# A burst's share of P @ V blocks in a two-branch attention kernel: from a rule on the queue's length to a rule on blocks left over runs left

## Chip, cores, metric

One core of a Trainium2 chip. The metric is device microseconds of one execution; before the change the median of 3 runs is 1779.55 us (1779.37 to 1779.65). Lower is better.

## What is computed

Two attention branches over the same 2048 x 512 input, mixed by a gate, in float32 throughout:

```python
x = A_x                                    # (1, 2048, 512), 32 heads of 16
g = sigmoid((x * gate_w).sum(-1, keepdims=True))
# branch A: softmax attention over all 2048 keys
a = (softmax(q @ k.T * 0.25) @ v) @ wo
# branch B: 4 segments of 512; causal softmax inside a segment,
# plus a linear memory M, z of the segments before it
o = sigmoid(beta) * (phi(q) @ M / (phi(q) @ z + 1e-6)) + (1 - sigmoid(beta)) * (softmax(causal logits) @ v)
b = o @ B_wo
return g * a + (1 - g) * b
```

## The kernel before, in words

**Two stages.** A first stage (up to about 300 us of the profile) makes the projections and the memory terms and leaves q, k and v of all heads in DRAM. The second stage is one loop over **slots**, written out by hand: the loop's order is the order of each engine's instructions.

**Units.** The work of the second stage is 64 units: a group of four heads and 512 queries, of branch A or B. Unit k (0 to 31) of A has 64 slots, that of B ten; they alternate (A 0, B 0, A 1, B 1, ...), 74 slots to a pair, 2368 slots in all. One slot of A is one head's 128 keys by 512 queries.

**What a slot n does**, in this order. `score_part` issues one score product `st<-qA,kA` on TensorE into one of three PSUM banks, and the exponential of it on ScalarE (`p<-st`), which writes a quarter of a tile `p` (128 keys, four heads, 512 queries). When four slots have filled such a tile, its four **blocks** (128 keys x 128 queries, four heads each) go into `queue`; for A they may be taken from slot n + 2 on (`GAP`). `max_part` works 96 slots ahead (`LEAD`): it makes the plain product `sm<-kA,qA` of a later unit into one of four PSUM banks (`banks[m % 4]`), and VectorE reduces it to the row maximum (`pm<-sm`, L226). For B it uses a masked reduce (L238, `rest<-sm,mask`), over one or two pieces to a slot. The softmax's shift is needed before a unit's scores can start, hence the lead.

**Bursts.** After every third slot (`BURST = 3`) comes the rest of TensorE's work: one of

- three products of `shared`, a list of the output projection and of later q tiles (about four bursts to a unit),
- or `some_values(n, most())`: P @ V blocks from the queue. `most()` says how many. Neighbouring blocks of one `p` tile are merged to a **run** of 128, 256, 384 or 512 columns: `ops<-p,vA`, four products (one to a head, in four column groups of the array; the profile counts eight records to a run). A run never goes beyond a `p` tile, so three blocks are one run or two (1+2, 2+1), four are 4, 1+3, 2+2 or 3+1.

So a burst on TensorE reads: three `st`, three `sm`, and the runs. Once to a pair of units a burst also carries the transposes of the maxima (`mt_ps<-identf,ms`, L196), which take one of the three score banks.

**The rule that the change touches**, L1008 to L1015. `ends` gives the shares by the number of blocks left near a unit's end (A: 9 left, take 3; 8, 4; 7, 3; 6, 3; 5, 5), and B's shares. Otherwise a burst takes 3, or 4 where `over` is true: the queue longer than `LOW = 3` by a share of `HIGH - LOW = 11` that shrinks with the unit's blocks left (for B: longer than 3). The last 94 slots (`wide`) and what follows them take up to 8 blocks at a time and do not ask the rule.

**Kinds of unit.** 74 slots are not a multiple of 3, so the bursts fall on a unit's slots in three ways, by k mod 3. Bursts of units with the same k mod 3 are alike; below, units 10, 11 and 12 stand for the three kinds (k mod 3 = 1, 2, 0), ten of each from unit 1 to unit 30.

Of the kernel before, what the change touches and what calls it, by code (L numbers as in the profile page):

```python
# [32 lines left out]
SLOTS = {"A": 64, "B": 10}  # L33
NU = 32
LEAD = 96
BURST = 3
LATER = (2, 3)
MOST = 3
LOW, HIGH = 3, 14
NP = 6  # L40
GAP = {"A": 2, "B": 5}
LATE_T = 9
# [5 lines left out]
def gated_mix(ctx, tc, x, xT, wqkv, a_wo, b_wq, b_wk, b_wv, b_wo, beta, gate_w, out):  # L48
# [55 lines left out]
    first = {}  # L104
# [5 lines left out]
    nS = len(slots)  # L110
# [138 lines left out]
    def run_todo(m):  # L249

        for e in [e for e in todo if e[0] <= m]:
            todo.remove(e)
            e[1]()

    def run_late(pool, tag, m):
        while us := [e for e in late if e[0] < m][:2]:
            for e in us:
                late.remove(e)
            transpose_max(us, pool, tag)
# [3 lines left out]
    def loads(m):  # L263

        m = min(m, len(maxs) - 1)
        while loaded[0] <= m:
            u, (r, i) = maxs[loaded[0]]
            if loaded[0] == first_max[u]:
                load_q(u)
            kc = u[2] if u[0] == "B" else i // 8  # L270
            if (u, kc) not in kt_:
                load_k(u, kc)
            loaded[0] += 1
# [383 lines left out]
    def later_tile(c, o):  # L657

        def done():
            full = fr.tile([128, CH], F32, tag="part", name="full")  # L660
            nc.scalar.copy(full, ops)
            t = fr.tile([128, 2, 2, 2, 128], F32R, tag="blk", name="qhalves", bufs=2)
            t = t.rearrange("p a o h t -> p a (o h t)")
            nc.gpsimd.tensor_copy(t[:, 0], full)
            nc.gpsimd.tensor_sub(t[:, 1], full, t[:, 0].bitcast(F32))
            for i in range(2):
                at(n + 12, lambda i=i: nc.sync.dma_start(
                    qd["A", o, c][16 * i:16 * i + 16].rearrange("d h t -> (d h) t"), raw(t[:, i])))


            if o == NO - 1 and c == LATER[0]:
                for i in range(2):
                    load_halves(("x", LATER[1]), "B", x_later(LATER[1]), (2 * i, 2 * i + 1), n + 2 + 18 * i,
                                [n + 24 + 29 * i, n + 28 + 29 * i])
            elif o == NO - 1:
                for i, (side, w) in enumerate((("A", a_wo), ("B", b_wo))):
                    load_halves(side, side, w, (0, 1), n + 2 + 18 * i, [n + 22 + 8 * i, n + 26 + 8 * i])
                    for k in range(2, 4):
                        load_halves(side, side, w, (k,), n + 50 + 22 * i + 3 * (k - 2), [n + 62 + 18 * i + 5 * (k - 2)])

        def f(i):
            k, (a, b) = i // 3, ((1, 0), (0, 1), (0, 0))[i % 3]
            assert {("q", k), (("x", c), k)} <= ready
            nc.tensor.matmul(ops, halved["q"][:, k, a, o * 128:(o + 1) * 128], halved["x", c][:, k, b],  # L684
                             start=(i == 0), stop=(i == 11))
            if i == 11:
                done()
        for i in range(12):
            yield lambda i=i: f(i)
# [30 lines left out]
    wide = range(nS - LEAD + 2, nS - 4)  # L720
    assert wide.start % (2 * BURST) == wide.stop % (2 * BURST) == 0

    def from_bank(n):

        return nc.vector.tensor_copy if n > wide.start + 4 else nc.scalar.copy

    queue = []

    def score_part(n):
# [38 lines left out]
        if j % 4 == 3 or j == SLOTS[side] - 1:  # L768
            if side == "B":
# [7 lines left out]
              + [(2, 0, 256), (2, 128, 384)])  # L777

    def some_values(n, most):

        taken = len(queue)
        while queue and most and queue[0][0] <= n:
            _, u, i = queue.pop(0)
            most -= 1
            side, g, c = u
            w = 1
            while (queue and most and queue[0][0] <= n and queue[0][1] == u and (i + w) // 4 == i // 4
                   and (side == "A" or PIECES[i + w][0] == PIECES[i][0])):
                queue.pop(0)
                most -= 1  # L790
                w += 1
            p = pt_[u, i // 4]
            if side == "A":
                c0 = q0 = 128 * (i % 4)
                v = vt[u][:, i // 16, i // 4 % 4]
            else:
                b, c0, q0 = PIECES[i]
                v = vt[u][:, b]
            done = i + w == SLOTS[side]
            for h in range(4):  # L800
                nc.tensor.matmul(ops[32 * h:32 * h + 17, q0:q0 + 128 * w], v[:, 17 * h:17 * h + 17], p[:, h, c0:c0 + 128 * w],  # L801
                                 start=(i == 0), stop=done, tile_position=(0, 32 * h))
            if done:
                raw = ob.tile([128, CH], F32, tag="o", name="oraw")
                from_bank(n)(raw, ops)
                nc.sync.dma_start(od[side, c][4 * g:4 * g + 4].rearrange("h r t -> (h r) t"), raw)
                stored.add(u)
                if side == "B" and c and g % 2 == 0:
                    octet("M", g // 2, c, n + 4)
                if (side, g ^ 1, c) in stored and u != ("A", NG - 1, NCH - 1):  # L810
                    octet(side, g // 2, c, n + (20 if side == "B" and (g < 5 or c < last) else 8))
                if u in between:
                    shared.extend(output(*between[u]))
                if side == "A" and c == 0:
                    shared.extend(later_tile(LATER[g // NO], g % NO))
                break
        return taken - len(queue)
# [117 lines left out]
    def output(c, b, pairs, then, ps=ops):  # L935

        ks = [(os, o, i) for os in pairs for o in os for i in range(2)]
        for k in ks:
            def f(n, k=k):
                os, o, i = k  # L940
                assert loaded_blocks[c, b, os] > len(blocks) - 2
                t = blocks[loaded_blocks[c, b, os] - 1][:, i, o % 2].unsqueeze(1)
                list(products(ps, t, 0, "AB"[i], o, k == ks[0], k == ks[-1]))[n]()
                if k == ks[-1] and n == 2:
                    then(ps, c, b)
            for n in range(3):
                yield lambda n=n, f=f: f(n)
# [57 lines left out]

    ends = {"A": {9: 3, 8: 4, 7: 3, 6: 3, 5: 5}, "B": {10: 3, 7: 3, 4: 4}}

    def most():  # L1008

        if not queue:  # L1010
            return 0
        side = queue[0][1][0]
        left = SLOTS[side] - queue[0][2]
        over = 64 * (len(queue) - LOW) > (HIGH - LOW) * (left if side == "A" else 0)
        return ends[side].get(left, MOST + over)  # L1015

    filled = [0]
    n = 0
    while n < nS or queue or beside or filled[0] < len(fill):
        for f in beside.pop(n, []):  # L1020
            f()
        if n < nS:
            score_part(n)
        m = n + LEAD
        if m < nS:
            loads(m + PRE)

            max_part(m, lambda: banks[m % 4])
        run_todo(m)
        if n >= nS or n % (2 * BURST if n in wide else BURST) == (2 * BURST if n in wide else BURST) - 1:  # L1030
            taken = 0
            if shared:
                for _ in range(3):
                    shared.pop(0)()
            else:
                taken = some_values(n, 8 if n >= nS or n in wide else most())
            if n < 5:


                for i in range(4):  # L1040
                    nc.tensor.matmul(ops[:, 128 * i:128 * i + 128], identf, identf, start=True, stop=True)
            if any(e[0] < m + 1 for e in late):
                run_late(st_ps, "st", m + 1)
            else:

                for _ in range(0 if n >= nS and queue else 4 if n not in wide else 11 - taken if taken < 8 else 0):
                    if filled[0] == len(fill) or fill[filled[0]][0] > n:
                        break
                    fill[filled[0]][1]()
                    filled[0] += 1  # L1050
        n += 1
# [45 lines left out]
```

## Time and profile before

| | |
|---|---|
| median of 3 runs | 1779.55 us (1779.37 to 1779.65) |
| profiled execution, its own time | 1779.57 us |
| its span, first to last instruction | 1777.8 us |
| PE (TensorE matmul) busy | 1770.5 us, 14945 records |
| PEld (weight loads) busy | 915.2 us |
| DVE (VectorE) busy | 1573.5 us |
| ACT (ScalarE) busy | 1435.4 us |
| POOL (GpSimd) busy | 641.2 us |
| granted TensorE clock | 1.000 |

The span is 1.8 us shorter than the execution's time; the profiled execution lies 0.02 us from the median. "Busy" is the union of an engine's instructions in time. Matmuls overlap each other, and so do VectorE's reduces (one starts before the last has written its result), so a row "4.27 ... x7" says that seven reduces took 4.27 us from the first one's start to the last one's end. In rows of the timeline the first number is the start of a group in us, the second its length, and "x" the number of instructions merged in it.

### The profile page before, as it was taken

The page shows a single profiled execution, that of the slowest core. Times are in us where ns is not written, and L with a number is a line of the kernel's source. Part 1 is how long each engine was busy: PE and PEld are TensorE (multiplying, and loading weights), DVE is VectorE, ACT ScalarE, POOL GpSimd, SP SyncE. Part 2 cuts the span into 40 slices and gives each one's busy share as a digit, 9 for nine tenths or more (in the row PEclk, how much of TensorE's full clock was granted, in tenths as well). Part 3 has the DMA queues.
Part 4 walks back from the last instruction along what each step waited for, and adds up shares of the span by engine and source line. Part 5 has one row for each costly group of instructions (what it writes and reads, how often), then busy time and mean ns, then how long its engine had stood idle before and what let it go on. Part 6 is the DMA issues. An engine that isn't in the chain of part 4 may idle for free.

```text
span 1777.8 us, 40673 instructions
## 1 busy us (share of the span) xinstructions
PE 1770.5 (100%) x14945; PEld 915.2 (51%) x14945; DVE 1573.5 (89%) x3331; ACT 1435.4 (81%) x2752; POOL 641.2 (36%) x748
## 2 busy tenths in 40 slices
PE   9999999999999999999999999999999999999999
PEld 8887776444444444444444444444444444444444
DVE  4236777999999999999999999999999999999931
ACT  5455445888888888888888888888888888888884
POOL 3002223415161417443434343344434253435343
PEclk9999999999999999999999999999999999999999
DMA  7667566445453536555454544454545353544542
GB/s 251 212 234 239 182 205 187 121 110 134 128 152 107 147 108 179 143 146 128 132 143 121 145 127 146 128 146 126 147 112 154 113 141 116 150 119 138 144 160 62
DMA packets 141270, 261.55 MB, mean 147 GB/s; under 512 B 36328, under 2 KB 58888, under 8 KB 140560
## 3 DMA queue, kind: packets, MB, share of 16 engines
q1 hardware_dynamic: 139712, 257.55, 50.3%
q8 instruction: 119, 1.95, 0.5%
q0 software_dynamic: 1216, 1.14, 0.3%
q14 instruction: 79, 0.65, 0.1%
q10 hardware_dynamic: 144, 0.26, 0.0%
HBM read 174.39 MB, written 83.25 MB: 145 GB/s over the span
## 4 chain that ended last, share of the span: by engine, by line
PE 95%; DVE 1%; ACT 1%; DMA 1%; POOL 1%; issue 0%; SPq 0%; POOLq 0%; DVEq 0%
PE ops L801 33%; PE st L744 27%; PE sm L205 14%; PE pr L311 10%; PE ops L913 4%; PE ops L684 2%; PE sm L913 2%; PE num L514 1%; POOL mn L378 1%; PE pr L401 1%; PE mps L545 0%; DVE pm L226 0%; DMA qdB<-q 0%; PE mt_ps L196 0%; DMA raw<-xT 0%; PE sm L744 0%
## 5 line engine op out<-in xcount | busy, mean ns | idle before, releaser
L767 ACT ACTIVATE p<-st 128x512 f32<-128x512 f32 x2261 | 1189.5, 601 | 152.3 <-PE sm L205 108.2
L226 DVE TENSOR_REDUCE pm<-sm 128x1 f32<-128x512 f32 x2048 | 1281.1, 683 | 11.5 <-PE sm L205 11.3
L744 PE MATMUL st<-qA,kA 50*128 50x512 f32 x2014 | 663.4, 432 | 0.0
L205 PE MATMUL sm<-kA,qA 48*128 48x512 f32 x2048 | 660.4, 428 | 0.4
L801 PE MATMUL ops<-p,vA 128*17 128x128 f32 (+3 forms) x6432 | 552.0, 442 | 0.0
L744 PEld LDWEIGHTS st<-qA,kA 50*128 50x128 f32 x2014 | 328.0, 185 | 415.1 <-ACT p L767 370.6
L205 PEld LDWEIGHTS sm<-kA,qA 48*128 48x128 f32 x2048 | 331.7, 185 | 16.9 <-issue 4.6
L863 POOL TENSOR_TENSOR rcp<-rec,minus 128x32 f32<-128x32 f32 x43 | 234.2, 5446 | 76.4 <-DMA rec<-dend 71.8
L238 DVE CUSTOM_DVE_ANT_0 rest<-sm,mask 128x128 f32<-128x128 f32 (+3 forms) x512 | 247.3, 483 | 1.4
L801 PEld LDWEIGHTS ops<-p,vA 128*17 128x17 f32 x6432 | 130.5, 96 | 214.4 <-issue 189.4
L748 POOL TENSOR_SCALAR_AFFINE_SELECT p<-p 128x512 f32<-128x512 f32 x128 | 79.4, 636 | 324.9 <-ACT p L767 320.4
L205 PE MATMUL sm<-kB,qB 48*128 48x128 f32 (+3 forms) x512 | 166.2, 385 | 0.0
L744 PE MATMUL st<-qB,kB 50*128 50x512 f32 (+1 forms) x495 | 109.3, 330 | 0.3 <-ACT mt L199 0.3
L381 DVE TENSOR_TENSOR q<-full,q 128x512 fp32r<-128x512 f32 x56 | 38.6, 689 | 74.9 <-ACT q L374 67.9
L744 PEld LDWEIGHTS st<-qB,kB 50*128 50x128 f32 x495 | 69.9, 186 | 59.3 <-ACT p L767 48.6
L801 PE MATMUL ops<-p,vB 128*17 128x128 f32 (+3 forms) x1504 | 87.5, 350 | 0.0
L205 PEld LDWEIGHTS sm<-kB,qB 48*128 48x128 f32 x512 | 80.0, 184 | 0.0
L187 POOL CAST ms<-nm 128x16 fp32r<-128x16 f32 x32 | 6.3, 196 | 201.5 <-DVE nm L183 199.6
L378 POOL TENSOR_SCALAR mn<-full 128x512 f32<-128x512 f32 x24 | 36.4, 1515 | 102.5 <-ACT full L373 82.2
L373 ACT COPY full<-pr 128x512 f32<-128x512 f32 x56 | 32.8, 586 | 40.2 <-PE pr L311 37.3
L187 POOL CAST ms<-pm 128x16 fp32r<-128x16 f32 x32 | 6.3, 196 | 127.9 <-DVE pm L238 127.8
L801 PEld LDWEIGHTS ops<-p,vB 128*17 128x17 f32 x1504 | 33.1, 97 | 31.1 <-issue 26.6
(198 smaller groups left out, 1622.7 us busy)
## 6 DMA issues: line engine op xcount, KB each, us to landing
kA<-kdA SPq DMA_DIRECT2D x256, 128.0 KB
vA<-vdA SPq DMA_DIRECT2D x31, 544.0 KB
kA<-kdA SPq DMA_DIRECT2D x256, 64.0 KB
kdA<-q SPq DMA_DIRECT2D x32, 256.0 KB
qdB<-q SPq DMA_DIRECT2D x32, 256.0 KB
qA<-qdA SPq DMA_DIRECT2D x64, 128.0 KB
kdB<-q SPq DMA_DIRECT2D x32, 256.0 KB
qB<-qdB SPq DMA_DIRECT2D x64, 128.0 KB
```

The source lines that it names most:

```text
L205: nc.tensor.matmul(ps[:, n0:n0 + n], rows(qt[u][:, :, s * 128:(s + 1) * 128], h, 48), rows(k[:, :, k0:k0 + n], h, 48), start=True, stop=True)
L226: nc.vector.tensor_reduce(pm[:, h, s, kc:kc + 1], ps, axis=AX.X, op=ALU.max)
L238: rows_left.append(lambda h=h, s=s, n0=n0, w=w: nc.vector.tensor_tensor_reduce(out=tri["rest"][:, 0:w], in0=ps[:, n0:n0 + w], in1=tri["mas ...
L311: nc.tensor.matmul(ps, l(a, k), r(b, k), start=(n == 0), stop=(n == 11))
L378: nc.gpsimd.tensor_scalar_min(ph["mn"], full, 0.0)
L381: nc.vector.tensor_sub(q2, full, q1.bitcast(F32))
L744: nc.tensor.matmul(ps[:, n0:n0 + CH - q0], rows(k[:, :, b * 128:(b + 1) * 128], h, 50), rows(q[:, :, q0:], h, 50), start=True, stop=True)
L748: nc.gpsimd.affine_select(out=x, in_=x, pattern=[[0, 4], [1, 128]], base=0, channel_multiplier=-1, compare_op=ALU.is_ge, fill=0.0)
L767: nc.scalar.activation(p[:, h], ps, AF.Exp, scale=SCALE)
L801: nc.tensor.matmul(ops[32 * h:32 * h + 17, q0:q0 + 128 * w], v[:, 17 * h:17 * h + 17], p[:, h, c0:c0 + 128 * w], start=(i == 0), stop=done ...
L863: eng.tensor_tensor(r, rec, minus, op=ALU.pow)
L913: yield lambda i=i, x=x, w=w: nc.tensor.matmul(ps, t[:, b, x], halved[side][:, o, w], start=start and i == 0, stop=stop and i == 2)
```

## The change

`most` now gets the slot n. For a unit of A it counts the bursts left until the unit's blocks should be done (`runs`, from the unit's first slot, its 64 slots and the gap) and takes four blocks where the blocks left but four are at least 3.5 times these bursts, and where more than six blocks (`due`) will have come in by the next burst, or it is the last. Else it takes three. The table `ends` holds only for B and when no burst is left, so for A it hardly applies any more. For B the share is as before. `HIGH` goes.

```diff
-LOW, HIGH = 3, 14
+LOW = 3
...
-    def most():
+    def most(n):
 
         if not queue:
             return 0
-        side = queue[0][1][0]
-        left = SLOTS[side] - queue[0][2]
-        over = 64 * (len(queue) - LOW) > (HIGH - LOW) * (left if side == "A" else 0)
-        return ends[side].get(left, MOST + over)
+        _, u, done = queue[0]
+        side, left = u[0], SLOTS[u[0]] - done
+        runs = (first[u] + SLOTS[side] + GAP[side] + 1 - n) // BURST
+        if side == "B" or runs < 1:
+            return ends[side].get(left, MOST + (len(queue) > LOW))
+        due = min(SLOTS[side], (n + BURST - GAP[side] - first[u] + 1) // 4 * 4) - done
+        return MOST + (left - 4 >= (MOST + 0.5) * runs and (due > 2 * MOST or runs == 1))
...
-                taken = some_values(n, 8 if n >= nS or n in wide else most())
+                taken = some_values(n, 8 if n >= nS or n in wide else most(n))
```

On ScalarE, VectorE, GpSimd and in the DMA queue of SyncE every instruction stands where it stood; only names of buffers and source lines differ. On TensorE the score products, the products for the maxima, the transposes, `shared` and B's runs stay in their bursts, and only the division of A's blocks among the bursts changes. Blocks per P @ V burst of A, in order ("t": the burst with the transposes):

| unit | before | after |
|---|---|---|
| 10 | 4 3 4 4 4 3 3 4 4 3 4 4 4t 3 3 2 4 4 | 4 4 3 4 3 4 3 4 3 4 3 4 3t 4 3 3 4 4 |
| 11 | 4 4 3 4 4 4 3 4 4 4 3 4 3t 4 3 3 2 4 | 4 4 3 4 3 4 3 4 3 4 3 4 3t 4 3 4 3 4 |
| 12 | 4 4 4 4 4 4 4 3 4 4 4 3t 3 3 4 4 4 | 4 4 4 4 4 4 4 4 4 3 4 3t 3 3 4 4 4 |

Over the whole loop up to `wide`, A's bursts of four go from 351 to 330, of three from 174 to 216, of two from 21 to 1 (547 bursts before and after). Its runs go from 220, 208, 168 and 208 (of 512, 384, 256 and 128 columns; 804 in all) to 229, 189, 188 and 189 (795).

TensorE in unit 11, from the fourth of its bursts above to the fifth (`st` scores of the running unit, `sm` products for the maxima of later ones, `ops` the runs); before:

```order
L801 MATMUL ops<-p,vA 17x128 x4
L801 MATMUL ops<-p,vA 17x384 x4
L744 MATMUL st<-qA_8967,kA_197 128x512
L205 MATMUL sm_3008<-kB_201,qB_9666 128x512
L744 MATMUL st<-qA_8967,kA_197 128x512
L205 MATMUL sm_3009<-kA_195,qA_9598 128x512
L744 MATMUL st<-qA_8967,kA_197 128x512
L205 MATMUL sm_3010<-kA_195,qA_9598 128x512
L801 MATMUL ops<-p,vA 17x128 x4
L801 MATMUL ops<-p,vA 17x384 x4
```

The same place after the change:

```order
L801 MATMUL ops<-p,vA 17x128 x4
L801 MATMUL ops<-p,vA 17x384 x4
L744 MATMUL st<-qA_8967,kA_197 128x512
L205 MATMUL sm_3008<-kB_201,qB_9654 128x512
L744 MATMUL st<-qA_8967,kA_197 128x512
L205 MATMUL sm_3009<-kA_195,qA_9586 128x512
L744 MATMUL st<-qA_8967,kA_197 128x512
L205 MATMUL sm_3010<-kA_195,qA_9586 128x512
L801 MATMUL ops<-p,vA 17x128 x4
L801 MATMUL ops<-p,vA 17x256 x4
```

The burst's second run has 256 columns in place of 384: three blocks, where there were four.

TensorE near the end of unit 11, its last burst but two and its last but one (the second `sm` of the piece belongs to B's maxima); before:

```order
L801 MATMUL ops<-p,vA 17x128 x4
L801 MATMUL ops<-p,vA 17x256 x4
L744 MATMUL st<-qA_8967,kA_199 128x512
L205 MATMUL sm_3008<-kB_200,qB_10319 128x256 x2
L744 MATMUL st<-qA_8967,kA_199 128x512
L205 MATMUL sm_3009<-kA_197,qA_10238 128x512
L744 MATMUL st<-qB_9666,kB_201 128x512
L205 MATMUL sm_3010<-kA_197,qA_10238 128x512
L801 MATMUL ops<-p,vA 17x256 x4
```

After:

```order
L801 MATMUL ops<-p,vA 17x384 x4
L801 MATMUL ops<-p,vA 17x128 x4
L744 MATMUL st<-qA_8967,kA_199 128x512
L205 MATMUL sm_3008<-kB_200,qB_10315 128x256 x2
L744 MATMUL st<-qA_8967,kA_199 128x512
L205 MATMUL sm_3009<-kA_197,qA_10234 128x512
L744 MATMUL st<-qB_9654,kB_201 128x512
L205 MATMUL sm_3010<-kA_197,qA_10234 128x512
L801 MATMUL ops<-p,vA 17x384 x4
```

The first burst of the piece grows from three blocks to four, the last from two to three: here the blocks go that were taken out of the bursts in the middle of the unit.

## The prediction

> **What bounds the kernel now.** I read the busy time by stretches first (PE, PEld, DVE, ACT, POOL, each with its instructions, then granted clock, DMA share, GB/s):
>
> ```profile
> 120.00:300.00 180.00, 179.01 (x844) 130.80 (x843) 126.04 (x239) 86.87 (x153) 45.00 (x42) 1.00 0.63 208
> ...
> 400.00:600.00 200.00, 199.97 (x1888) 91.29 (x1890) 199.80 (x423) 176.77 (x343) 74.24 (x90) 1.00 0.50 133
> ...
> 1400.00:1600.00 200.00, 200.00 (x1887) 91.39 (x1886) 199.74 (x423) 177.17 (x344) 82.01 (x92) 1.00 0.50 133
> 1600.00:1660.00 60.00, 60.00 (x580) 27.27 (x576) 59.89 (x123) 52.77 (x103) 24.32 (x28) 1.00 0.50 144
> ```
>
> In the slot loop both PE and DVE read 100%, so this view cannot say which of them sets the pace; ACT (88%) and the weight loads (46%) do not. Next I read the timeline of PE in unit 11 for the price of a burst, from the start of its runs to the next `st`, and from one first `st` to the next.
>
> ```profile
> 816.63 0.50 PE L744 MATMUL st<-qA,kA 50*128 50x512 f32 x1
> ...
> 817.53 0.84 PE L801 MATMUL ops<-p,vA 128*17 128x384 f32 x8
> 818.30 0.50 PE L744 MATMUL st<-qA,kA 50*128 50x512 f32 x1
> ...
> 819.28 1.06 PE L801 MATMUL ops<-p,vA 128*17 128x128 f32 x16
> 820.27 0.50 PE L744 MATMUL st<-qA,kA 50*128 50x512 f32 x1
> ...
> 824.95 0.85 PE L801 MATMUL ops<-p,vA 128*17 128x128 f32 x16
> 825.72 0.49 PE L744 MATMUL st<-qA,kA 50*128 50x512 f32 x1
> ...
> 826.65 1.06 PE L801 MATMUL ops<-p,vA 128*17 128x256 f32 x16
> 827.64 0.50 PE L744 MATMUL st<-qA,kA 50*128 50x512 f32 x1
> ```
>
> Three blocks in one run take 0.77 us (817.53 to 818.30), as 1+2 too 0.77 (824.95 to 825.72); four as 1+3 take 0.99 (819.28 to 820.27), as 2+2 again 0.99. So **the price goes by blocks, about 0.22 us each, and hardly by runs**. From `st` to `st` a burst of three costs 1.67 us (816.63 to 818.30), one of four 1.92 (825.72 to 827.64).
>
> Then the timeline of DVE in the same unit:
>
> ```profile
> 819.62 1.28 DVE L226 TENSOR_REDUCE pm<-sm 128x1 f32<-128x512 f32 x2
> 820.84 0.69 DVE L238 CUSTOM_DVE_ANT_0 rest<-sm,mask 128x512 f32<-128x512 f32 x1
> ...
> 821.46 9.91 DVE L226 TENSOR_REDUCE pm<-sm 128x1 f32<-128x512 f32 x16
> ...
> 831.41 4.27 DVE L226 TENSOR_REDUCE pm<-sm 128x1 f32<-128x512 f32 x7
> 835.68 0.29 DVE L238 CUSTOM_DVE_ANT_0 rest<-sm,mask 128x128 f32<-128x128 f32 x1
> ```
>
> One reduce lasts 0.69 us, but seven last 4.27: their starts lie (4.27 - 0.69) / 6 = 0.597 apart. That is DVE's own pace, 1.79 us for three, between PE's 1.67 and 1.92. Sixteen at that pace would last 0.69 + 15 x 0.597 = 9.65; they last 9.91. DVE was **starved for 0.26 us inside a row that shows it busy throughout**, because the tail of one reduce covers the wait for the next. That is what bounds the loop: DVE at its pace, plus such starved stretches where PE comes with bursts of four and has no lead left. The four `sm` banks are the lead: a burst of four eats 0.13 of it, one of three gives 0.12 back. In unit 11 the sequence before is 4 3 4 4 4 3 4 4 4 over this stretch.
>
> **The change, part by part.** Nothing is added and no other engine's order moves; A's blocks go to other bursts. TensorE's sum is the same: 42 more bursts of three, 21 fewer of four and 21 fewer of two, and 0.22 us a block makes that nothing. What counts is where a four stands on spent lead.
>
> *Unit 11's kind.* Starved now: 0.26 in the row of sixteen; and seven reduces from 831.41 should end their turn at 831.41 + 7 x 0.597 = 835.59, but the next starts at 835.68: 0.09. Together 0.35. After the change fours and threes alternate from the third burst on, so each four (-0.13) meets a three (+0.12) before it, and the lead entering the stretch, which fed the first fours, is kept. Both waits go. What was moved out goes into its last bursts but two and but one, 3 2 becoming 4 3. The 0.02 at 820.84 (1.22 for two starts that need 1.19) stays: the bursts ahead of it are unchanged.
>
> *Unit 10's kind.*
>
> ```profile
> 775.46 10.33 DVE L226 TENSOR_REDUCE pm<-sm 128x1 f32<-128x512 f32 x17
> ...
> 785.83 3.67 DVE L226 TENSOR_REDUCE pm<-sm 128x1 f32<-128x512 f32 x6
> 789.46 0.29 DVE L238 CUSTOM_DVE_ANT_0 rest<-sm,mask 128x128 f32<-128x128 f32 x1
> ...
> 790.75 0.69 DVE L226 TENSOR_REDUCE pm<-sm 128x1 f32<-128x512 f32 x1
> 791.50 0.29 DVE L238 CUSTOM_DVE_ANT_0 rest<-sm,mask 128x128 f32<-128x128 f32 x1
> ```
>
> Seventeen should last 10.24: 0.09 starved. Six from 785.83 should end at 789.41, the next starts 789.46: 0.05. From 790.75 to 791.50 is 0.75 in place of 0.60: 0.15, behind the burst that carried four blocks and the transposes. Sum 0.29. After the change this burst carries three, and three ahead of it are no longer 4 4 4. All of it goes.
>
> *Unit 12's kind.*
>
> ```profile
> 865.73 1.28 DVE L226 TENSOR_REDUCE pm<-sm 128x1 f32<-128x512 f32 x2
> 867.00 0.69 DVE L238 CUSTOM_DVE_ANT_0 rest<-sm,mask 128x512 f32<-128x512 f32 x1
> ...
> 867.62 9.31 DVE L226 TENSOR_REDUCE pm<-sm 128x1 f32<-128x512 f32 x15
> ...
> 876.97 3.07 DVE L226 TENSOR_REDUCE pm<-sm 128x1 f32<-128x512 f32 x5
> 880.13 0.29 DVE L238 CUSTOM_DVE_ANT_0 rest<-sm,mask 128x128 f32<-128x128 f32 x1
> ```
>
> Here seven fours stand in a row, and the change makes them nine; it then takes a three where the last four but one stood. Now: 0.08 at 867.00 (1.27 for 1.19), 0.26 in the fifteen (9.31 for 0.69 + 14 x 0.597 = 9.05), which is three starved bursts at 0.09, and 0.175 at 880.13 (3.16 for 5 x 0.597). The first two stay. Two further fours cost 2 x 0.09 = 0.175; the three that now stands later restores lead and the 0.175 at 880.13 goes. Net 0. Bounds: +0.175 a unit if the later three restores all and the further fours cost nothing; -0.26 if nothing comes back and each further four costs the whole 0.13. I take 0, since starved rows carry 0.09.
>
> **Sum.** Each kind comes ten times, and the waits repeat to 0.01 us:
>
> ```profile
> 365.59 10.33 DVE L226 TENSOR_REDUCE pm<-sm 128x1 f32<-128x512 f32 x17
> ...
> 1641.25 9.91 DVE L226 TENSOR_REDUCE pm<-sm 128x1 f32<-128x512 f32 x16
> ```
>
> 10 x (0.35 + 0.29 + 0) = 6.4 us. The profiled execution took 1779.57 us (span 1777.8), 0.02 from the median; the forecast is 1779.57 - 6.4 = **1773.2 us**. Its own range: 1.75 more if unit 12's kind gains its bound, 1771.4; and half of the 6.4, with unit 12's kind at its worst (2.6), 1779.0.
>
> **Rivals.**
>
> *Nothing is left to gain (1779.6).* DVE's 199.80 of 200 us says that the loop is full, and a wait taken away in one place could return in the next. The Trainium skill (Perfetto Trace Analysis, Identifying the Most-Contended Engine) calls occupancy a fair measure for Vector of how close it is to its limit; by that rule the loop has 0.1% to give and the time stays. The trace disagrees: busy throughout, sixteen reduces took 0.614 apart and seven 0.597. Against the rival too: the waits sit only where fours follow each other, and DVE's total work is fixed.
>
> *PE alone is the bound, and runs have a price of their own (1777.2).* The groups of A's runs:
>
> ```profile
> L801 PE MATMUL ops<-p,vA 128*17 128x512 f32 x1760 | 232.3, 598 | 0.0
> L801 PE MATMUL ops<-p,vA 128*17 128x384 f32 x1664 | 173.6, 489 | 0.0
> L801 PE MATMUL ops<-p,vA 128*17 128x256 f32 x1344 | 98.7, 382 | 0.0
> L801 PE MATMUL ops<-p,vA 128*17 128x128 f32 x1664 | 85.2, 277 | 0.0
> ```
>
> With eight records to a run, a run costs 1.06, 0.83, 0.59 and 0.41 us busy. The new counts change by +9, -19, +20 and -19: +9.5 - 15.9 + 11.8 - 7.8 = -2.4 us. For it: PE reads 100%, and the chain that ended last runs over PE. Against it: 1+3, 2+2 cost the same 0.99 in the timeline; busy time of short runs overlaps. The Trainium skill (Perfetto Trace Analysis, Matmuls) says that larger matmuls are more efficient than smaller ones; by it nine fewer runs would be the whole gain, and the burst rows do not bear it out.
>
> *A block waits for its exponential (slower, 1784.7).* PE takes blocks in order; if a burst reaches one whose exponential is not done, all `st` and `sm` behind it wait, then DVE. The trace has this at the last four of unit 12:
>
> ```profile
> 889.57 1.29 PE L801 MATMUL ops<-p,vA 128*17 128x512 f32 x8
> ...
> 890.79 0.50 PE L744 MATMUL st<-qB,kB 50*128 50x512 f32 x1
> ```
>
> 1.22 us to the next `st` in place of 0.99: 0.23. Five bursts of the table grow from the tenth on in units 10 and 11, where the queue is shortest. If all wait so: 50 x 0.23 = 11.5, less 6.4, gives +5.1. It decides from 0.13 each. Against: added up, the blocks taken by any burst are never ahead of before in unit 11, and by one block at most in units 10 and 12.
>
> *The change doesn't do what it says.* "No run of two" is not so: runs of 256 columns rise from 168 to 188. What goes is bursts of two blocks (21 to 1). By blocks this is the forecast, by runs the second rival.
>
> **How the numbers follow.** Forecast 0.75, run widths 0.08, nothing 0.10, slower 0.07. From 1771.4 to 1777.6 lie the forecast but for its upper end and the second rival; nothing and slower, 0.17, are left out. A difference of 0.2% (3.6 us) is about what can be told from no change: faster than 1776.0 takes the forecast but for 0.07, so 0.68; within 0.2%: 0.07 + 0.08 + 0.10 = 0.25; slower 0.07.
>
> **What would show it.** In a unit of kind 11 the sixteen reduces last 9.65 in place of 9.91; in kind 10 the seventeen 10.24, and the start after the transposes comes 0.60 behind its forerunner; in kind 12 the row of fifteen grows by about 0.17, while the five from 876.97 lead over without 0.175. Bursts of four keep 0.99. Wrong would be: the same rows unchanged (nothing), rows right but waits of the same size at the unit's end, or runs of 1.29 us in many bursts (the third rival).

## The result, and the profile after

| | before | after |
|---|---|---|
| median of 11 runs on one chip | 1779.65 us (1779.0 to 1781.19) | 1775.4 us (1775.09 to 1776.58) |
| profiled execution | 1779.57 us | 1775.26 us |
| its span | 1777.8 us | 1773.5 us |

The changed kernel is 4.25 us faster: a ratio of 0.9976, with an interval of 0.9968 to 0.9984. The forecast was 6.4 us faster, 1773.2; the measured time lies inside the range given, 1771.4 to 1777.6. So the direction held, the size did not: two thirds of the forecast gain came. The mechanism held in the rows that were forecast; as an account of what bounds the whole loop it said too much (below).

The busy time by stretches of the changed kernel (PE, PEld, DVE, ACT, POOL, granted clock, DMA share, GB/s):

```profile
400.00:600.00 200.00, 200.00 (x1882) 91.02 (x1883) 199.89 (x423) 177.54 (x344) 73.81 (x89) 1.00 0.49 134
...
1400.00:1600.00 200.00, 200.00 (x1863) 90.38 (x1854) 199.92 (x424) 177.47 (x344) 81.54 (x92) 1.00 0.49 136
```

Nothing shows here, as nothing did before: both engines read full while the loop became shorter. The gain has to be looked for in the starts of VectorE's reduces. The timeline of DVE in the changed kernel, units 10, 11 and 12 one after the other:

```profile
774.18 10.26 DVE L226 TENSOR_REDUCE pm<-sm 128x1 f32<-128x512 f32 x17
...
784.46 3.69 DVE L226 TENSOR_REDUCE pm<-sm 128x1 f32<-128x512 f32 x6
788.16 0.29 DVE L238 CUSTOM_DVE_ANT_0 rest<-sm,mask 128x128 f32<-128x128 f32 x1
...
789.45 0.69 DVE L226 TENSOR_REDUCE pm<-sm 128x1 f32<-128x512 f32 x1
790.05 0.28 DVE L238 CUSTOM_DVE_ANT_0 rest<-sm,mask 128x128 f32<-128x128 f32 x1
...
790.25 0.69 DVE L226 TENSOR_REDUCE pm<-sm 128x1 f32<-128x512 f32 x1
...
819.94 9.66 DVE L226 TENSOR_REDUCE pm<-sm 128x1 f32<-128x512 f32 x16
...
829.63 4.28 DVE L226 TENSOR_REDUCE pm<-sm 128x1 f32<-128x512 f32 x7
833.93 0.29 DVE L238 CUSTOM_DVE_ANT_0 rest<-sm,mask 128x128 f32<-128x128 f32 x1
...
865.88 9.49 DVE L226 TENSOR_REDUCE pm<-sm 128x1 f32<-128x512 f32 x15
...
875.41 3.07 DVE L226 TENSOR_REDUCE pm<-sm 128x1 f32<-128x512 f32 x5
878.40 0.29 DVE L238 CUSTOM_DVE_ANT_0 rest<-sm,mask 128x128 f32<-128x128 f32 x1
```

The long rows came out as forecast: seventeen at 10.26 (10.24 forecast), sixteen at 9.66 (9.65), fifteen at 9.49 (9.31 + 0.17), and the start behind the transposes in unit 10 after 0.60 (790.05 less 789.45). In unit 12 the wait after the five is gone: 878.40 less 875.41 is 2.99, five starts at 0.597. One thing did not: in units 10 and 11 **the wait just ahead of the first masked reduce stands**. Six reduces from 784.46 should lead over at 788.04, and 788.16 is 0.12 late (0.05 before); seven from 829.63 should at 833.81, and 833.93 is 0.12 late (0.09 before).

Measured over whole units, from the start of the first maximum of a unit's third burst to that of the next unit's (unit 11: 810.02 to 854.26 before, 808.51 to 852.53 after), mean of the ten units of a kind (nine of unit 12's, whose last runs into `wide`):

| kind | forecast | measured |
|---|---|---|
| of unit 10 | -0.29 | -0.236 us |
| of unit 11 | -0.35 | -0.165 us |
| of unit 12 | 0 | +0.004 us |

Times ten, this is 4.0 us of the 4.3 between the two profiled executions.

TensorE's bursts show the same gain from the other side. Time from the start of the first burst named to the start of the one behind the last, mean of the ten units of a kind:

| kind, its bursts of A's blocks | blocks before, after | before | after |
|---|---|---|---|
| 10, first to twelfth | 44, 43 | 21.89 us | 21.84 us |
| 10, thirteenth (transposes) | 4, 3 | 2.15 | 1.92 |
| 10, the last five | 16, 18 | 9.20 | 9.23 |
| 11, first to tenth | 38, 36 | 18.56 | 18.33 |
| 11, eleventh to fifteenth | 17, 17 | 9.10 | 9.12 |
| 11, the last three | 9, 11 | 5.57 | 5.61 |

Two more blocks at a unit's end cost 0.03 and 0.04 us there, where the blocks alone would cost 0.44: before, TensorE waited at that place. The burst behind the one of two blocks took 2.18 us in unit 10, held up by an exponential for 0.28, and 2.39 in unit 11, held up by one of VectorE's masked reduces:

```profile
844.47 0.19 PEld L205 LDWEIGHTS sm<-kA,qA 48*128 48x128 f32 x2 [0.34 <-DVE pm L238]
```

All waits of this kind over 0.15 us in the whole execution (us in total, times, longest), before and after:

```profile
PEld sm L205 <- DVE pm L238: 4.0, 13, 0.5
```

```profile
PEld sm L205 <- DVE pm L238: 1.1, 4, 0.5
```

The nine that went stood 136.6 us apart, one to a unit of kind 11 (the first at 434.61, the last at 1527.70). So the change takes blocks from bursts in which VectorE waits for TensorE and puts them where TensorE waited for others. And in the first ten bursts of kind 11, two blocks less bring 0.23 us, not 0.44: 0.2 is lost there again.

### The profile page after: what moved, and what is told of

Same layout as the page of the kernel before. It is cut to its first block, busy times and chain, and to the rows that moved or that the text cites. A ratio compares the mean times of both kernels' runs of the same rounds, so it can differ in the third digit from the quotient of the medians.

```text
span 1773.5 us, 40529 instructions
## 1 busy us (share of the span) xinstructions
PE 1766.7 (100%) x14873; PEld 911.8 (51%) x14873; DVE 1570.9 (89%) x3331; ACT 1437.2 (81%) x2752; POOL 641.1 (36%) x748
## 4 chain that ended last, share of the span: by engine, by line
PE 95%; DVE 1%; DMA 1%; ACT 1%; POOL 1%; issue 0%; SPq 0%; POOLq 0%; ACTq 0%
PE ops L801 33%; PE st L744 27%; PE sm L205 14%; PE pr L311 10%; PE ops L913 4%; PE ops L684 2%; PE sm L913 2%; PE num L514 1%; POOL mn L378 1%; PE pr L401 1%; DMA raw<-xT 1%; PE mps L545 0%; DVE pm L226 0%; DMA qdB<-q 0%; PE mt_ps L196 0%; PE sm L744 0%
## 5 line engine op out<-in xcount | busy, mean ns | idle before, releaser
L226 DVE TENSOR_REDUCE pm<-sm 128x1 f32<-128x512 f32 x2048 | 1281.3, 687 | 11.5 <-PE sm L205 11.2
L801 PE MATMUL ops<-p,vA 128*17 128x256 f32 (+3 forms) x6360 | 552.0, 445 | 0.0
L238 DVE CUSTOM_DVE_ANT_0 rest<-sm,mask 128x128 f32<-128x128 f32 (+3 forms) x512 | 248.3, 485 | 0.4
L879 POOL TENSOR_TENSOR v<-v,inv 128x512 f32<-128x512 f32 x31 | 39.9, 1286 | 28.1 <-DMA inv<-rdA 24.2
```

The lines of the kernel that those rows point to most:

```text
L226: nc.vector.tensor_reduce(pm[:, h, s, kc:kc + 1], ps, axis=AX.X, op=ALU.max)
L238: rows_left.append(lambda h=h, s=s, n0=n0, w=w: nc.vector.tensor_tensor_reduce(out=tri["rest"][:, 0:w], in0=ps[:, n0:n0 + w], in1=tri["mas ...
L879: eng.tensor_mul(k["v"], k["v"], k["inv"])
```

## The experiments

All are compared with the kernel before on the same chip. Its median was 1779.98 us beside the three runs by kind and the exchange of ninth and tenth share; 1779.72 beside the exchange of tenth and eleventh and the three runs on what bounds the loop; 1779.85 beside the version that follows and the loads four steps earlier; 1779.95 beside the control and the two small products. Differences to the changed kernel are taken by way of these: its own is -4.25.

### One kind at a time: three runs

The rule of before stays, and the units of one kind get the changed kernel's shares from a table: kind 10 in the first run, 11 in the second, 12 in the third.

```diff
+SHARE = {1: (4, 4, 3, 4, 3, 4, 3, 4, 3, 4, 3, 4, 3, 4, 3, 3, 4, 4)}
...
+        u = queue[0][1]
+        k = NG * u[2] + u[1]
+        if u[0] == "A" and 0 < k < NU - 1 and k % 3 in SHARE:
+            bursts[u] = bursts.get(u, -1) + 1
+            return SHARE[k % 3][bursts[u]]
```

In the second run the table's line is

```diff
+SHARE = {2: (4, 4, 3, 4, 3, 4, 3, 4, 3, 4, 3, 4, 3, 4, 3, 4, 3, 4)}
```

and in the third

```diff
+SHARE = {0: (4, 4, 4, 4, 4, 4, 4, 4, 4, 3, 4, 3, 3, 3, 4, 4, 4)}
```

Expected of kind 10 alone:

> The kernel before, with the new shares in units of kind 10 alone (k mod 3 = 1). Lead theory: VectorE's starved time of this kind goes, 0.24 us a unit by the two traces, ten units: 2.4 us faster than before. Run-width theory: this kind's runs by the busy time of their groups change by +0.5 us: no gain. Nothing-to-gain theory: 0.

Expected of kind 11 alone:

> The kernel before, with the new shares in units of kind 11 alone (k mod 3 = 2). Lead theory: 0.17 us a unit by the two traces, 1.7 us faster than before. Run-width theory: +0.7 us: no gain.

Expected of kind 12 alone:

> The kernel before, with the new shares in units of kind 12 alone (k mod 3 = 0): nine bursts of four in a row. Lead theory: two more starved bursts (+0.18 us) and one wait before the transposes less (-0.18), so 0 within 0.5 us. Run-width theory: twenty fewer runs, -3.8 us, nearly the whole gain of the change.

| kind changed alone | median | to before | ratio, interval | per unit of the kind |
|---|---|---|---|---|
| 10 | 1777.45 us | -2.53 | 0.9987 (0.9978 to 0.9995) | -0.235 |
| 11 | 1778.46 us | -1.52 | 0.9991 (0.9982 to 1.0) | -0.183 |
| 12 | 1780.24 us | +0.26 | 1.0003 (0.9994 to 1.0012) | about 0 |

The last column is from the traces, as in the table above; by the times alone, kind 11's interval reaches 1.0 and kind 12's holds it. The gain lies where the lead of VectorE says, and adds up: -2.53 - 1.52 + 0.26 = -3.8, of 4.25. Widths of runs would have given the opposite order, most of it in kind 12. And kind 11, forecast to bring most, brings less than kind 10, by itself too: no other kind's bursts are to blame.

### The tenth burst

The wait that stayed comes right behind the tenth burst of a unit. In kinds 10 and 11 it is the burst in which a new unit's first products for the maxima begin. TensorE in unit 11 of the changed kernel, an ordinary four behind a three (from 824.00) and then the tenth burst (from 827.58):

```profile
824.00 0.50 PE L744 MATMUL st<-qA,kA 50*128 50x512 f32 x1
...
824.58 0.41 PE L205 MATMUL sm<-kA,qA 48*128 48x512 f32 x1
824.92 1.06 PE L801 MATMUL ops<-p,vA 128*17 128x384 f32 x16
825.90 0.50 PE L744 MATMUL st<-qA,kA 50*128 50x512 f32 x1
...
827.58 0.50 PE L744 MATMUL st<-qA,kA 50*128 50x512 f32 x1
...
828.28 0.47 PE L205 MATMUL sm<-kA,qA 48*128 48x512 f32 x1
828.68 1.05 PE L801 MATMUL ops<-p,vA 128*17 128x512 f32 x8
829.66 0.50 PE L744 MATMUL st<-qA,kA 50*128 50x512 f32 x1
```

The ordinary one takes 1.90 us from `st` to `st`, the tenth 2.08 (2.09 in the mean of its kind). The four blocks cost 0.98 in both; the 0.18 is lost ahead of them, between the first score and the third `sm` (0.58 and 0.70) and from there to the blocks (0.34 and 0.40). In the kernel before, the same burst has a four ahead of it, and takes 1.88:

```profile
829.52 0.49 PE L744 MATMUL st<-qA,kA 50*128 50x512 f32 x1
...
830.42 1.06 PE L801 MATMUL ops<-p,vA 128*17 128x256 f32 x16
831.40 0.50 PE L744 MATMUL st<-qA,kA 50*128 50x512 f32 x1
```

### Ninth and tenth share exchanged

The changed kernel, with a table for kinds 10 and 11 ahead of its rule:

```diff
+SHARE = {1: (4, 4, 3, 4, 3, 4, 3, 4, 4, 3, 3, 4, 3, 4, 3, 3, 4, 4), 2: (4, 4, 3, 4, 3, 4, 3, 4, 4, 3, 3, 4, 3, 4, 3, 4, 3, 4)}
```

The tenth burst is now a three behind a four.

> The changed kernel, with the ninth and tenth shares exchanged in kinds 10 and 11 (... 3 4 3 4 becomes ... 4 3 3 4), so that the burst that brings a new unit's first products for the maxima carries three blocks and does not come behind a three. Spent-lead theory for the wait left at the transposes (0.11 us in both kinds, after a burst of four that took 2.09 us): the wait goes, about 0.1 us in 20 units, 1.5 to 2 us faster than the changed kernel. Rival, that this wait is a thing of the burst itself and no lead removes it: 0, or slower by up to 0.5 us for two fours that now follow each other.

1774.25 us, ratio 0.9968 (0.9956 to 0.998): 5.7 us under before, 1.5 more than the change. VectorE in unit 11 (L228 and L240 are the L226 and L238 of the others):

```profile
820.78 9.72 DVE L228 TENSOR_REDUCE pm<-sm 128x1 f32<-128x512 f32 x16
...
830.54 4.27 DVE L228 TENSOR_REDUCE pm<-sm 128x1 f32<-128x512 f32 x7
834.72 0.29 DVE L240 CUSTOM_DVE_ANT_0 rest<-sm,mask 128x128 f32<-128x128 f32 x1
```

The wait is gone (4.18 for seven), so the tenth burst is where it came from. The two fours now side by side cost 0.07 in the sixteen (9.72): the remainder of the same account.

### Tenth and eleventh exchanged, and an earlier three in kind 12

```diff
+PRE = 20; SHARE = {1: (4, 4, 3, 4, 3, 4, 3, 4, 3, 3, 4, 4, 3, 4, 3, 3, 4, 4), 2: (4, 4, 3, 4, 3, 4, 3, 4, 3, 3, 4, 4, 3, 4, 3, 4, 3, 4), 0: (4, 4, 4, 4, 3, 4, 4, 4, 4, 3, 4, 3, 4, 3, 4, 4, 4)}
```

> The changed kernel with shares written out: kinds 10 and 11 as changed but with the tenth and eleventh exchanged (... 3 4 3 4 becomes ... 3 3 4 4, no fours ahead of the new unit's first products), kind 12 as 4 4 4 4 3 4 4 4 4 3 4 3t 4 3 4 4 4 (one three moved from behind the transposes to the middle of the row of fours). Lead theory: kinds 10 and 11 lose the 0.11 us wait at the transposes without starving elsewhere, about 2 to 2.5 us; in kind 12 a three in the row of fours saves some 0.2 us a unit and up to 0.1 comes back at its end, 1 to 2 us; together 3 to 4.5 us faster than the changed kernel, near 1772 us. Rival (shares only move the waits about): within 1 us of the changed kernel.

1774.66 us, ratio 0.997 (0.9958 to 0.9981), 0.8 better than the change: **a miss**. I had taken it that a three in the tenth burst is enough. TensorE in unit 11:

```profile
827.49 0.50 PE L744 MATMUL st<-qA,kA 50*128 50x512 f32 x1
...
828.59 0.84 PE L801 MATMUL ops<-p,vA 128*17 128x384 f32 x8
829.36 0.50 PE L744 MATMUL st<-qA,kA 50*128 50x512 f32 x1
```

A tenth burst of three takes 1.87 in place of 1.67 when a three stands ahead, and the wait stays. Of the 3 to 4.5 us expected 0.8 came, which is what the rival said. Together with the runs before, the mean tenth burst of kind 11 reads:

| | is a four | is a three |
|---|---|---|
| behind a four | 1.89 (before) | 1.67 (exchange of nine and ten) |
| behind a three | 2.09 (changed) | 1.87 (this run) |

So a three **ahead** costs 0.2 us here, whatever the burst itself carries. (In kind 10 the tenth burst before is a three behind a four, and takes 1.67.) VectorE is not what holds it: in the run below that halves its reduces, the tenth burst takes 2.09 too. In kind 12 the three that now stands in the row of fours brought 0.08 a unit, of 0.1 to 0.2 expected.

### A three behind a four: the version that follows

```diff
+PRE = 20; SHARE = {1: (4, 4, 3, 4, 3, 4, 3, 3, 4, 3, 4, 4, 3, 4, 3, 3, 4, 4), 2: (4, 4, 3, 4, 3, 4, 3, 3, 4, 3, 4, 4, 3, 4, 3, 4, 3, 4), 0: (4, 4, 4, 4, 3, 4, 4, 4, 4, 3, 4, 3, 4, 3, 4, 4, 4)}
```

Two threes stand side by side where they cost nothing (seventh and eighth), the ninth is a four, the tenth a three.

> The changed kernel with another order of the same shares: in kinds 10 and 11 shares eight to eleven become 3 4 3 4, so that the tenth burst, the one that brings a new unit's first products for the maxima, is a three and has a four ahead of it, and no two fours stand together before it; kind 12 as in e5_shares. If the burst's length is set by how many blocks stand ahead of it (a three ahead costs 0.2 us there), the tenth burst takes about 1.67 us, the wait at the masked reduces of the transposes' burst goes, and the sixteen reduces before stay near 9.65 us: about 0.4 us a unit in kind 10, and more in kind 11, so 1772 to 1773.2 us, 6.5 to 7.7 us under the kernel before and 1 to 2 us under e4_swap. Rival: the blocks only move the wait to the next burst that has none to spare: 1774 us or more, as in e5_shares.

1771.98 us, ratio 0.9956 (0.9943 to 0.9968): **7.9 us under before, 3.6 more than the change**. The table's forecast was 6.5 to 7.7 under. Its VectorE in unit 11:

```profile
818.29 9.65 DVE L226 TENSOR_REDUCE pm<-sm 128x1 f32<-128x512 f32 x16
...
827.99 4.26 DVE L226 TENSOR_REDUCE pm<-sm 128x1 f32<-128x512 f32 x7
832.17 0.28 DVE L238 CUSTOM_DVE_ANT_0 rest<-sm,mask 128x128 f32<-128x128 f32 x1
```

Both waits of unit 11 are at zero: what the forecast asked of the change is to be had, by another order of the same shares. Kinds 10 and 11 gain 0.36 a unit each over before (0.4, and more in kind 11, were expected), kind 12 gains 0.08.

### Why a three ahead costs 0.2: late tiles?

```diff
-PRE = 20
+PRE = 24
```

> The changed kernel with the loads of a unit issued four steps earlier (PRE 24 for 20), nothing else. If the tenth burst of kinds 10 and 11 is long because the new unit's q and k tiles come late, its 2.09 us fall to about 1.89, the wait of about 0.11 us at the masked reduces behind goes in twenty units, and the kernel is about 2 us faster than the changed one. If it is long because of what stands ahead of it on TensorE's queue and ScalarE (exponentials of a burst of three back to back with its own), nothing changes: within 0.5 us of the changed kernel, tenth burst at 2.09.

The tenth burst stays at 2.08, so the tiles do not come late. But the time is 1787.93 us, ratio 1.0053 (1.0039 to 1.0067), **12 us above the changed kernel**: neither theory had that. By the start of the same maxima, 3.2 us are lost before the loop begins (304.02 to 307.24 for its first), of which 1.1 stand already at the first maximum of all (165.07 to 166.16), where the control below is 1.0 late too; nothing is lost in the loop (1256.4 and 1256.1 us from slot 152 to slot 2200), and 9.7 us are lost near its end. TensorE there:

```profile
1665.53 0.97 PE L913 MATMUL ops<-wA,blk 128*128 128x512 f32 x3
...
1671.19 0.55 PE L744 MATMUL st<-qB,kB 50*128 50x256 f32 x1 [4.25 <-DMA kB<-kdB]
...
1672.88 1.65 PE L913 MATMUL ops<-wB,blk 128*128 128x512 f32 x3
```

The last k tile of B is late by 4.25 us, and afterwards the same three products take 1.65 in place of 0.97, in a stretch with a mean granted clock of 0.56 (in the changed kernel it is 1.00 there):

```profile
1671.00:1685.00 14.00, 13.65 (x62) 7.47 (x66) 8.61 (x25) 7.40 (x14) 4.00 (x3) 0.56 0.23 68
```

As a control, the same four steps for the loop's loads alone, without the first stage and without the last 400 slots:

```diff
-            loads(m + PRE)
+            loads(m + PRE + 4 * (m < nS - 400))
```

> The changed kernel with the loads of the slot loop alone four steps earlier, but not in the first stage and not in the last 400 steps. If what e10_pre24 lost lies in those two places, where the earlier loads collide with others, this kernel is within 1 us of the changed one, with the tenth burst at 2.09 as before. Rival (earlier loads cost in the loop too): 3 us or more above it.

1775.91 us, ratio 0.9979 (0.997 to 0.9988): 4.0 under before, the changed kernel's time within 0.3. Its tenth burst in unit 11 runs from 828.45 to 830.53, 2.08. Earlier tiles do nothing here, and what the run above lost lay outside the loop.

### Why a three ahead costs 0.2: waits in the queue?

A new unit's first two products wait on four DMA queues each; TensorE's queue carries these waits as four instructions (`EVENT_SEMAPHORE`), two to a product, that only wait. Of unit 11's tenth burst in the changed kernel, these instructions (ns: shortest, median, longest; first and last start):

```profile
L205 PEldq EVENT_SEMAPHORE  x4: 51/51/51, 827.6 to 828.2; - x4
```

and the weight loads of TensorE, an ordinary burst first, the tenth from 827.58 on:

```profile
824.49 0.18 PEld L744 LDWEIGHTS st<-qA,kA 50*128 50x128 f32 x1 [0.19 <-ACT p L767]
824.50 0.18 PEld L205 LDWEIGHTS sm<-kA,qA 48*128 48x128 f32 x1
824.91 0.13 PEld L801 LDWEIGHTS ops<-p,vA 128*17 128x17 f32 x8 [0.24 <-issue]
...
828.07 0.18 PEld L744 LDWEIGHTS st<-qA,kA 50*128 50x128 f32 x1
828.25 0.18 PEld L205 LDWEIGHTS sm<-kA,qA 48*128 48x128 f32 x1
828.67 0.13 PEld L801 LDWEIGHTS ops<-p,vA 128*17 128x17 f32 x8 [0.24 <-issue]
```

Behind a three, the third score of a burst is held until its bank's exponential is done, 0.49 us after the burst's start in both (824.00 to 824.49, 827.58 to 828.07). In the ordinary burst the third `sm` follows at once (0.01), and the burst takes 1.90, so the hold alone costs nothing. In the tenth two of the four waits stand behind the held score (828.06 and 828.17), the third `sm` comes 0.18 later, and the blocks with it (0.42 and 0.60 from the third score's load to theirs). To take these waits away from this place, the next run issues two small products (128 of 512 columns) with the new unit's tiles a burst earlier, into banks that the slot's own product then overwrites, with the loop's loads as in the control:

```diff
             kc, s, h = i // 8, i % 8 // 2, 2 * r + i % 2
+            v = maxs[m + 3][0] if m > LEAD and m + 3 < nS else u
+            if v[0] == "A" and v != u and m + 3 - first_max[v] in (0, 1):
+                max_product(ps, v, 2 * r, 0, 0, 128, kt_[v, 0])
...
-            loads(m + PRE)
+            loads(m + PRE + 4 * (m < nS - 400))
```

> The changed kernel with two small products of the new unit's q and k (128 of 512 columns each, into the banks that the slot's own product then overwrites) one burst ahead of the tenth, and the loop's loads four steps earlier so that the tiles are there by then. The eight queue waits of the new unit (four at each of its first two products) then stand in the burst before, a three behind a four. Theory (the waits stand in TensorE's queue behind a score that is held up by its exponential): the tenth burst of kinds 10 and 11 takes about 1.90 us in place of 2.09, and the wait at the masked reduces behind it goes; the burst before grows by the two products, some 0.1 to 0.2 us, so the time stays within 2 us of the changed kernel. Rival (the exponentials of the burst of three alone set it): the tenth burst stays at 2.09, and the time is 1 to 4 us above the changed kernel for the added products.

TensorE in unit 11, the burst before the tenth and the tenth:

```profile
829.42 0.50 PE L747 MATMUL st<-qA,kA 50*128 50x512 f32 x1
...
831.20 0.50 PE L747 MATMUL st<-qA,kA 50*128 50x512 f32 x1
...
832.10 1.05 PE L804 MATMUL ops<-p,vA 128*17 128x512 f32 x8
833.08 0.49 PE L747 MATMUL st<-qA,kA 50*128 50x512 f32 x1
```

The tenth burst takes 1.88 in place of 2.08; the one before takes 1.78 for 1.67, with two products more. In unit 10's kind one of the small products falls into the tenth burst itself, which takes 1.99. The wait at the masked reduces shrinks to 0.04 in unit 11 and stays at 0.11 in unit 10. The time is 1776.68 us, ratio 0.9981 (0.9972 to 0.999), 0.8 above the control; from unit 2 to unit 29 both traces take the same (1226.1 and 1226.3 us), so the products cost what the waits did. By itself this run does not part the waits from the hold: as the burst before is 0.11 longer, the third score is held for 0.38 us in place of 0.49 (831.20 to 831.58). What parts them are the rows together:

| | held for 0.49 us | held for 0.34 to 0.38 |
|---|---|---|
| no waits | 1.90 (ordinary four behind a three) | 1.88 (tenth burst of this run) |
| four waits | 2.08 (changed) | 1.88 (before, behind a four) |

So neither costs by itself, and the 0.2 comes from both together: **waits that stand in TensorE's queue behind a held score**. Behind a four (before), the queue passes the first two while the blocks ahead still run (829.30, 829.42) and the other two at 829.80 and 829.90, and they cost nothing.

### What bounds the loop: three runs

No run over 256 columns:

```diff
-            while (queue and most and queue[0][0] <= n and queue[0][1] == u and (i + w) // 4 == i // 4
+            while (w < 2 and queue and most and queue[0][0] <= n and queue[0][1] == u and (i + w) // 4 == i // 4
```

> The changed kernel with the same blocks in every burst, but no run of more than 256 columns: a run of four becomes two of two, a run of three 2+1 or 1+2. Blocks theory: 2+2 costs 0.99 us as one run of four does (0.005 more), so 0 to 1.5 us slower than the changed kernel. Run-width theory: by the groups' busy time +58 us.

1777.15 us, ratio 0.9985 (0.9976 to 0.9994), 1.7 above the changed kernel. A's wide groups in the changed kernel,

```profile
L801 PE MATMUL ops<-p,vA 128*17 128x512 f32 x1832 | 241.9, 598 | 0.0
L801 PE MATMUL ops<-p,vA 128*17 128x384 f32 x1512 | 158.1, 490 | 0.0
```

are all split, 229 + 189 = 418 runs of A (34 of B). 1.7 us over 452 runs is 4 ns a run; each of the two times compared has an interval of about 1.5 us to either side, so 4 ns can hardly be told from nothing. The Trainium skill (Perfetto Trace Analysis, Matmuls) says that larger matmuls are more efficient; for these runs the measurement puts the size of it at 4 ns, in a loop that TensorE nearly bounds (below).

Three `sm` banks, so less lead:

```diff
-            max_part(m, lambda: banks[m % 4])
+            max_part(m, lambda: banks[m % 3])
```

> The changed kernel with three sm banks in the slot loop in place of four, nothing else. Lead theory: the banks are the lead; without the fourth nearly none can be kept, and every burst of four starves VectorE by 0.1 us or more: 30 to 60 us slower. If lead plays no part: 0.

1875.81 us, ratio 1.054 (1.0525 to 1.0554): 100 us above the changed kernel. The direction held; the size was over the 30 to 60 expected. Its waits, TensorE for VectorE and VectorE for TensorE (us in total, times, longest), show that each waits for the other in turn:

```profile
PEld sm L205 <- DVE pm L226: 52.3, 269, 0.4
...
DVE pm L226 <- PE sm L205: 25.0, 76, 2.1
```

Half of the columns left out of the reduce (so half of A's keys are left out of the softmax's shift):

```diff
-            nc.vector.tensor_reduce(pm[:, h, s, kc:kc + 1], ps, axis=AX.X, op=ALU.max)
+            nc.vector.tensor_reduce(pm[:, h, s, kc:kc + 1], ps[:, 0:CH // 2], axis=AX.X, op=ALU.max)
```

> The changed kernel with the maximum of branch A taken over 256 of each tile's 512 columns (half of the keys are left out of the shift), so that VectorE's reduce takes about half as long. If VectorE set the pace by far, the loop would fall towards ScalarE's 88%; lead theory with TensorE close behind: TensorE's own bursts add up to nearly the same time, what it waits for VectorE's banks goes (some 15 us at most), so 5 to 20 us faster and no more. If TensorE alone were the bound: 0.

1767.81 us, ratio 0.9932 (0.9918 to 0.9945): 7.7 under the changed kernel. One stretch of each, three banks first:

```profile
400.00:600.00 200.00, 200.00 (x1748) 100.48 (x1748) 192.68 (x403) 166.75 (x322) 68.51 (x85) 1.00 0.46 122
```

```profile
400.00:600.00 200.00, 200.00 (x1874) 90.27 (x1870) 133.49 (x423) 177.29 (x344) 71.37 (x93) 1.00 0.52 139
```

With a bank less, TensorE still reads 100%. With half the reduce, VectorE is busy for 133.49 of 200 us and no longer holds TensorE up; but of the 7.7 us most lie ahead of the loop's regular part. Starts of the same two maxima, one in unit 2 and one in unit 29:

| | unit 2 | unit 29 | between |
|---|---|---|---|
| before | 411.59 us | 1641.25 us | 1229.66 us |
| changed | 411.17 | 1637.33 | 1226.16 |
| changed, half the reduce | 406.68 | 1629.94 | 1223.26 |
| a three behind a four (whole reduces) | 410.86 | 1633.32 | 1222.46 |

4.5 us are gained before unit 2, and 2.9 of 1226 us in between. So in the changed kernel's loop TensorE's own bursts are the nearer bound, with 0.24% to VectorE's account; and the version that took 0.2 us from the tenth burst is faster there, with whole reduces, than the changed kernel with half of them.

## Why the prediction was right, and where its size failed

- **VectorE bounds the loop at its pace, plus starved stretches that a busy share doesn't show**: half right. The starved stretches are there, and the starts of reduces gave the gain row by row where the busy share stayed at 199.7 to 199.9 of 200. That VectorE's pace bounds the loop is too much: with its reduces halved, the changed kernel's loop is only 2.9 us of 1226 shorter. The two engines take turns. In the middle of a unit VectorE waits for TensorE's fours, at the end TensorE waits, in kind 11 for VectorE. The prediction put the blocks that go to the last bursts at no cost and gave no reason; what they cost there, 0.03 to 0.04 us for two, goes with these waits.
- **The price goes by blocks, not by runs**: right. Kind 12 alone gains nothing (+0.26, where run widths asked for -3.8), and 452 further runs cost 1.7 us (where they asked for 58). That rival falls.
- **Unit 12's kind, 0**: right, and by both its parts: the fifteen grew by 0.18 (0.17 forecast) and the 0.175 behind the five went.
- **Unit 10's kind, 0.29**: 0.236 measured. The rows: 0.07 in the seventeen (0.09 forecast) and 0.15 behind the transposes, as forecast; 0.06 more behind that, where the next reduce's start came 0.26 after the masked reduce (to 791.76) and now 0.20 (790.05 to 790.25); and 0.07 lost at the wait that should have gone and grew from 0.05 to 0.12. The start of that next reduce before:

```profile
791.76 0.69 DVE L226 TENSOR_REDUCE pm<-sm 128x1 f32<-128x512 f32 x1
```

- **Unit 11's kind, 0.35**: the mis-sized term, 0.165 measured, and the step that failed is "each four (-0.13) meets a three (+0.12) before it, and the lead entering the stretch, which fed the first fours, is kept. Both waits go." The first wait went (0.25 of 0.26). The second, 0.09, became 0.12: the prediction gave every burst of four the same 1.92 us, and the tenth burst took 2.09 as soon as a three stood ahead of it. Twenty units of the two kinds times the 0.12 that stayed are 2.4 us; the gain fell 2.15 short of the forecast. The version with a three behind a four took it away and more.
- **The exponentials as a rival**: it put the slower case at blocks that wait for their exponential. No row shown of after has that, but what cost the 0.18 is related: a score that waits for an exponential, with other waits queued behind it. The rival looked at the burst's runs, not at what stands between the burst's scores.
- **Nothing is left to gain** falls. By the rule of the Trainium skill (Perfetto Trace Analysis, Identifying the Most-Contended Engine), occupancy is a fair measure of how near Vector is to its limit. For a gain of this size it is too coarse here: VectorE read 199.7 to 199.9 of 200 before, after, and in the version that is 7.9 us (0.44%) faster.
- **The change does what it says**, by blocks: bursts of two go, and the gain lies in where threes and fours stand. (21 of them go, as the prediction's sum has it. The counts of the bursts before add up to 546 of 547; with 22 bursts of two in place of 21 they and the blocks come out.)

## What to carry to other kernels

Where two engines both read full, look at the starts of the same instruction in a row, per stretch: here 0.26 us too much in a row of sixteen showed where to look. Look then for the place where the other engine waits: blocks moved there cost 0.03 us for two in place of 0.44. When work is spread evenly over slots, a slot's price also depends on its neighbour: find the slots that carry waits for new tiles, and put the heavy slot ahead of them, so that the queue meets these waits while the engine works. A 2 x 2 table of one burst (itself and the one ahead) told this apart from four runs, and gave a version 3.6 us better than the rule. And a run that lightens one engine is read by stretch too: of its 7.7 us, 2.9 lay in the loop that was in question.

## What the runs showed of the hardware that was not expected

- Waits in TensorE's queue that are long fulfilled, at 51 ns each, cost 0.18 us for a burst where two of them stood behind a weight load held for 0.49 us; where they stood otherwise, and where a load was held so without them, the burst took 1.88 and 1.90 us.
- A stop of 4.25 us on TensorE was followed by 14 us at a mean granted clock of 0.56; by the starts of the same maxima that place cost 9.7 us in all.
- One bank of lead less cost 100 us (5.7% of the changed kernel). From 400 to 1650 us the mean burst of four went from 1.92 to 2.10 us, and that of three from 1.69 to 1.76.
